# A planner for five engines: GpSimd waits for VectorE at the shared ports, a narrower last values product, and a new table of order

## The chip, the cores and the metric

The kernel runs on one core of a Trainium2 chip. A core has engines that each work through a queue of their own in order: PE (TensorE, matrix products), DVE (VectorE), ACT (ScalarE), POOL (GpSimd) and SP (SyncE, which issues the DMA transfers). They wait for each other by semaphores. The metric is the device time of one execution in microseconds, as the median of several runs.

## What is computed

Attention in which each row keeps only its 32 largest scores, and two dense blocks behind it. All is in 32-bit floating point.

```python
batch, n_heads, seq, head_dim = (2, 8, 576, 64)
scores = scale * np.matmul(q, k.transpose(0, 1, 3, 2))
kth = np.partition(scores, -top_k, axis=-1)[..., -top_k:-top_k + 1]      # top_k = 32
scores = np.where(scores >= kth, scores, -1000000000.0)
scores = scores - np.max(scores, axis=-1, keepdims=True)
attn = np.exp(scores)
attn = attn / (np.sum(attn, axis=-1, keepdims=True) + 1e-09)
x = np.matmul(attn, v)                      # laid out as 1152 tokens x 512
h = x @ w_in                                # 512 -> 2048
sp = np.where(h > 20.0, h, np.log1p(np.exp(np.minimum(h, 20.0))))
x = (h * np.tanh(sp)) @ w_out               # 2048 -> 512
h = x @ w2_in
return (h * (1.0 / (1.0 + np.exp(-h)))) @ w2_out
```

## The kernel before

The 1152 tokens are 9 tiles of 128 rows. For each tile the 8 heads are taken two at a time, so there are 36 attention steps of one tile and two heads; this text calls them **pairs** and numbers them from 1 in the order in which their reciprocals stand in DVE's queue. For a pair PE multiplies queries and keys, both split into a high and a low part (`scores`, L378, into `ps_att`); ACT or DVE copies the scores to `sc`; DVE finds the 32 largest of each row by four rounds of MAX8 (L394) and MATCH_REPLACE8 (L397) for each head. For the first six tiles ACT then computes the exponentials (L410) and DVE masks them and sums them up in one operation, the **mask** (L414, a SCALAR_TENSOR_TENSOR of 128x576 with a sum; two for a pair); for the last three tiles the mask is made ahead of the exponential instead, by ACT (L420) and a difference on POOL or DVE (L290, L292). The sum becomes `den`: a constant is added on ACT (L462) or POOL (L463), DVE takes the **reciprocal** (L466), ACT spreads it (L469). PE transposes the exponentials (`turn`, L439, nine 128x128 pieces), multiplies them by the values (`values`, L455 and L457), transposes the reciprocals (L471), and DVE multiplies both (L480), which gives the pair's x.

The two dense blocks take the tiles in the groups of `BLOCK1` and `BLOCK2`. Groups marked 'n' multiply in the native 32-bit form (an instruction gives two records in the trace), those marked 'r' split both sides into high and low parts and make three products (L630, L701, L808). Weights arrive as 64-bit floats and are turned into 32-bit ones once (`convert`: ACT at L505 and L517, POOL at L509 and L519). `split_unit` splits the activated values into two parts, the second a difference on POOL (L290) or DVE (L292).

Nothing of this is issued in the order in which the code is written. Every step is handed to `Plan.add` with its ways (an engine, a cost, a rank offset and a function), what it reads and writes, and the buffers that it uses. `Plan.emit` then runs a small clock for each engine and always emits the step that can start first, by rank among equals; this order is the order of the queues on the chip. The ranks come from tables: `TILES`, `DUE1` and `DUE2` give start times of tiles and groups, `FLEX`, `FLEX1`, `EARLY` and `OFF` offsets for kinds of steps and for the choice of the engine.

DVE and POOL share ports to the on-chip memory. The planner marks the operations that use them (`way[4]`: every POOL operation, and on DVE the two-elements-a-cycle copies, the differences and the masks) and does not let two of them overlap in its own clock (`port`). On the chip nothing keeps that order before the change: POOL starts as soon as its data are there.

## Time and profile before

| | |
|---|---|
| runs | 652.88, 656.01, 656.37 us; median 656.01 |
| profiled execution | span 654.1 us from the first to the last instruction; no other time of its own is given |
| PE busy | 606.1 us, 93% |
| DVE busy | 539.5 us, 82% |
| ACT busy | 476.3 us, 73% |
| POOL busy | 382.3 us, 58% |
| granted TensorE clock, mean | 0.987 |

The span lies inside the spread of the runs and 1.9 us below their median. A share of busy time is an average over the whole span; the kernel begins with attention alone and ends with matrix products alone, so the shares of its stretches differ.

### The profile page before, as it was taken

The page shows a single profiled execution, that of the slowest core. Times are in us where ns is not written, and L with a number is a line of the kernel's source. Part 1 is how long each engine was busy: PE and PEld are TensorE (multiplying, and loading weights), DVE is VectorE, ACT ScalarE, POOL GpSimd, SP SyncE. Part 2 cuts the span into 40 slices and gives each one's busy share as a digit, 9 for nine tenths or more (in the row PEclk, how much of TensorE's full clock was granted, in tenths as well). Part 3 has the DMA queues.
Part 4 walks back from the last instruction along what each step waited for, and adds up shares of the span by engine and source line. Part 5 has one row for each costly group of instructions (what it writes and reads, how often), then busy time and mean ns, then how long its engine had stood idle before and what let it go on. Part 6 is the DMA issues. An engine that isn't in the chain of part 4 may idle for free.

```text
span 654.1 us, 13089 instructions
## 1 busy us (share of the span) xinstructions
PE 606.1 (93%) x4536; PEld 537.0 (82%) x4536; DVE 539.5 (82%) x1106; ACT 476.3 (73%) x993; POOL 382.3 (58%) x334
## 2 busy tenths in 40 slices
PE   1298788999999999999999999999999999999997
PEld 1177667999999866668999878999988899999996
DVE  4999999997999999989999979979998234554550
ACT  6799999988699998988978666878777344332321
POOL 6898569761267888987549236556787233322221
PEclk9999967999999999999999999999999999999999
DMA  8987649898789868799999589875876998887752
GB/s 309 293 256 222 197 159 330 312 361 263 204 271 345 276 192 271 268 305 347 389 402 368 151 272 355 316 259 191 272 255 223 374 300 294 278 263 256 246 179 80
DMA packets 85650, 178.34 MB, mean 273 GB/s; under 512 B 8144, under 2 KB 29136, under 8 KB 85584
## 3 DMA queue, kind: packets, MB, share of 16 engines
q1 hardware_dynamic: 85584, 177.50, 80.4%
q8 instruction: 36, 0.59, 0.3%
q14 instruction: 30, 0.25, 0.1%
HBM read 138.94 MB, written 38.54 MB: 271 GB/s over the span
## 4 chain that ended last, share of the span: by engine, by line
PE 53%; DVE 16%; ACT 15%; DMA 7%; issue 4%; POOL 4%; SPq 1%; POOLq 0%; ACTq 0%
PE ps_h L630 20%; PE ps_y L701 12%; PE ps_y L808 11%; DVE m L394 6%; DVE rest L397 5%; ACT ws L505 4%; PE ps_att L378 3%; DMA wraw<-w1i 3%; PE ps_att L439 2%; PE ps_misc L455 2%; ACT wraw L517 2%; ACT pt L282 2%; ACT e L410 2%; DVE e L414 2%; POOL wraw L519 2%
## 5 line engine op out<-in xcount | busy, mean ns | idle before, releaser
L394 DVE MAX8 m<-rest 128x8 f32<-128x576 f32 x216 | 154.4, 745 | 0.1
L397 DVE MATCH_REPLACE8 rest<-m,rest 128x576 f32<-128x576 f32 x144 | 106.2, 741 | 0.0
L509 POOL TENSOR_TENSOR ws<-ws 128x512 int32<-128x512 int32 x64 | 86.7, 1359 | 28.9 <-ACT ws L505 27.2
L378 PE MATMUL ps_att<-kk,qs 128*128 128x288 f32 x320 | 72.8, 346 | 31.6 <-POOL kk L290 24.5
L282 ACT CAST ws<-wraw 128x512 fp32r<-128x512 f32 x93 | 57.4, 621 | 53.8 <-PE ps_h L630 25.3
L519 POOL TENSOR_TENSOR wraw<-wraw,ws 128x512 int32<-128x512 int32 x64 | 85.5, 1346 | 15.9 <-ACT wraw L517 11.0
L505 ACT ACTIVATE ws<-wide,zone 128x512 int32<-128x512 int16 x128 | 94.5, 779 | 0.0
L378 PEld LDWEIGHTS ps_att<-kk,qs 128*128 128x128 f32 x320 | 51.3, 205 | 43.2 <-POOL kk L290 26.0
L292 DVE TENSOR_TENSOR ws<-wraw,ws 128x512 fp32r<-128x512 f32 x65 | 58.9, 924 | 31.3 <-ACT ws L282 30.9
L630 PE MATMUL ps_h<-y,ws 128*128 128x256 f32 x576 | 75.3, 280 | 0.0
L630 PEld LDWEIGHTS ps_h<-y,ws 128*128 128x128 f32 x576 | 73.1, 188 | 2.7
L290 POOL TENSOR_TENSOR ws<-wraw,ws 128x512 fp32r<-128x512 f32 x44 | 57.6, 1318 | 27.3 <-ACT ws L282 14.8
L630 PE MATMUL ps_h<-xt,ws 128*128 128x256 f32 x576 | 72.8, 282 | 0.0
L701 PE MATMUL ps_y<-wide,ws 128*128 128x256 f32 x540 | 71.3, 283 | 0.0
L630 PEld LDWEIGHTS ps_h<-xt,ws 128*128 128x128 f32 x576 | 69.5, 188 | 1.5 <-issue 1.2
L290 POOL TENSOR_TENSOR wide<-th,wide 128x512 fp32r<-128x512 f32 x24 | 31.5, 1313 | 66.7 <-DVE wide L284 65.4
L701 PEld LDWEIGHTS ps_y<-wide,ws 128*128 128x128 f32 x540 | 66.5, 189 | 0.0
L808 PE MATMUL ps_y<-ws,wide 128*128 128x512 f32 x252 | 64.8, 396 | 0.0
L290 POOL TENSOR_TENSOR wide<-hs,wide 128x512 fp32r<-128x512 f32 x24 | 32.0, 1342 | 49.4 <-DVE wide L284 40.2
L439 PE MATMUL ps_att<-ident,e 128*128 128x128 f32 x324 | 52.6, 287 | 6.7 <-DVE e L414 3.9
L701 PE MATMUL ps_y<-hs,wraw 128*128 128x128 f32 x384 | 52.4, 286 | 2.2 <-ACT hs L670 2.2
L394 DVE MAX8 m<-sc 128x8 f32<-128x576 f32 x72 | 52.8, 747 | 1.3 <-ACT sc L282 0.7
(89 smaller groups left out, 1231.5 us busy)
## 6 DMA issues: line engine op xcount, KB each, us to landing
wraw<-w1i SPq DMA_DIRECT2D x64, 256.0 KB, 4.8
wraw<-w2i SPq DMA_DIRECT2D x64, 256.0 KB, 4.0
ws<-w1o_split SPq DMA_DIRECT2D x30, 512.0 KB, 5.1
ws<-w2o_split SPq DMA_DIRECT2D x28, 512.0 KB, 4.4
wraw<-w1o SPq DMA_DIRECT2D x48, 256.0 KB, 5.8
wide<-in_w1i_dram SPq DMA_DIRECT2D x16, 512.0 KB, 5.6
wide<-in_w1o_dram SPq DMA_DIRECT2D x16, 512.0 KB, 5.0
wide<-in_w2i_dram SPq DMA_DIRECT2D x16, 512.0 KB, 5.1
```

What stands on the lines that cost most here:

```text
L282: ways.append(("act", act_us(n, psum), act, lambda: nc.scalar.copy(get_out(), get_in())))
L290: ways.append(("pool", pool_us(n), pool, lambda: nc.gpsimd.tensor_tensor(out=get_out(), in0=get_a(), in1=get_b(), op=op)))
L378: nc.tensor.matmul(o, lhsT=l, rhs=r[:, f * SH:(f + 1) * SH], start=(i == 0), stop=(i == len(ops) - 1))
L394: add([("dve", 0.67, 0, lambda i=i, h=h, src=src: nc.vector.max(out=m8()[:, h, 8 * i:8 * i + 8], in_=src()[:, h]))], reads=srck, writes=[K ...
L397: add([("dve", 0.73, 0, lambda i=i, h=h, src=src: nc.vector.match_replace(out=rest()[:, h], in_to_replace=m8()[:, h, 8 * i:8 * i + 8], in_ ...
L439: nc.tensor.transpose(o[:, i, :], ef[:, (c + i) * P:(c + i + 1) * P], ident)
L505: add([("act", act_us(UNIT) + 0.14, 0, lambda i=i: nc.scalar.activation(pn()[:, i], top(), AF.Relu, scale=ONE16 - 2 * ONE16 * i, bias=zone))],
L509: ways = [("pool", pool_us(UNIT), 0, lambda: nc.gpsimd.tensor_tensor(out=se(), in0=pn()[:, 0], in1=pn()[:, 1], op=ALU.subtract))]
L519: add([("pool", pool_us(UNIT), 0, lambda: nc.gpsimd.tensor_tensor(out=w().bitcast(I32), in0=w().bitcast(I32), in1=se(), op=ALU.add))], rea ...
L630: nc.tensor.matmul(hp[:, c, :], lhsT=l, rhs=rr, start=(i == 0), stop=(i == len(ops) - 1))
L701: nc.tensor.matmul(yp[:, o, :], lhsT=l[:, d * P:(d + 1) * P], rhs=rr[:, c, :], start=(fc == 0 and k == 0 and o == 0), stop=last, skip_grou ...
L808: nc.tensor.matmul(op, lhsT=gg[:, c, i * P:(i + 1) * P], rhs=wt, start=(fc == 0 and k == 0), stop=(fc == NFC - 1 and k == len(ops) - 1))
```

## The change

Five things are edited. First, `Plan.emit` keeps the last port operation of DVE (`turn_of`), and when the next port operation that it emits is POOL's, that one gets a dependency on it (`order`, which adds a semaphore wait); in the planner's clock POOL may use the port 0.13 us after DVE's end. A DVE operation behind a POOL operation gets none. Second, the last chunk of the values product, which holds the tails of both heads, is two matmuls with 64 columns of weights, one for each head, instead of one with 128. Third, the split activations get three buffers of their own, `g`, instead of sharing `wide` with the arriving weights. Fourth, some costs and ranks in the planner change, and the scratch for DMA descriptors is set to 1024 bytes. Fifth, all numbers of the tables are new.

```diff
-TILES = [(19.37, 6.76), (46.36, 14.1), (106.73, 4.63), (204.37, 9.99), (225.06, 11.69), (258.55, 49.85), (345.98,
+TILES = [(-38.49, 10.5), (10.1, 9.21), (77.14, -12.91), (164.62, 9.79), (162.43, 9.24), (220.65, 45.49), (300.21,
...
-                 wraw=9, ws=8, hs=2, th=1, wide=3, y=2, o=2)
+    wraw=9, ws=8, hs=2, th=1, wide=3, g=3, y=2, o=2)
...
-        dma, hw, port = 0.0, 0.4, 0.0
+        dma, hw = 0.0, 0.4
+        port, turn_of = dict(dve=0.0, pool=0.0), None
...
-                    if way[4] and port > at:
-                        at, soon = port, soon and port <= free[e] + PORT
+                    if way[4] and port[e] > at:
+                        at, soon = port[e], soon and port[e] <= free[e] + PORT
...
-            fn()
+            done = fn()
             free[e] = end
-            if shared:
-                port = end
+            if shared and e == "dve":
+                port["pool"], turn_of = end + self.WAIT[e], done
+            elif shared:
+                port["dve"] = end
+                if turn_of is not None:
+                    self.order(done, turn_of)
+                    turn_of = None
...
+    def order(after, before):
+        tc.add_manual_dep(after.ins, before.ins.name, mybir.DependencyInfo(mybir.DependencyClass.Sync, mybir.DependencyReason.DATA),
+                          reason="port")
...
-                nc.tensor.matmul(av[:, r0:r1], lhsT=v[:, 2 * NM:].rearrange("p c e -> p (c e)"), rhs=pt()[:, NM, r0:r1],
-                                 start=False, stop=True, skip_group_check=True)
-        add([("pe", 1.35 * len(pp), 0, values)], reads=[K("pt", c) for c in range(0, NB, 3)] + [("v", b, p) for b, _, _ in pp],
+                for h in range(2):
+                    nc.tensor.matmul(av[h * D:h * D + D, r0:r1], lhsT=v[:, 2 * NM + h, :], rhs=pt()[:, NM, r0:r1],
+                                     start=False, stop=True, skip_group_check=True)
+        add([("pe", 1.25 if len(pp) == 1 else 1.32, 0, values)], reads=[K("pt", c) for c in range(0, NB, 3)] + [("v", b, p) for b, _, _ in pp],
...
-        add([("act", 0.11, 0, lambda: nc.scalar.add(den()[:, 0], den()[:, 0], tiny)),
+        add([("act", 0.2, 0, lambda: nc.scalar.add(den()[:, 0], den()[:, 0], tiny)),
...
-            rank=rank - 6, boost="wsplit")
+            rank=rank - (6 if g else 2), boost="wsplit")
...
-        hi = lambda: get(key, lambda: sbuf("wide", [P, 2 * UNIT + 2], F32R)[:, :2 * n].rearrange(
-            "p (t n) -> p t n", t=2))[:, 0]
+        hi = lambda: get(key, lambda: sbuf("g", [P, 2, UNIT], F32R)[:, :, :n])[:, 0]
...
-    nc = _bacc.Bacc("TRN2", target_bir_lowering=False, num_devices=1)
+    nc = _bacc.Bacc("TRN2", target_bir_lowering=False, num_devices=1, dynamic_dma_scratch_size=1024)
```

What the tables move is seen in the queues. Three places follow. Lines of the changed kernel are 12 to 14 higher: its L407, L410, L427, L480, L494 and L801 are L394, L397, L414, L466, L480 and L788 of before.

DVE's queue around pair 20, before: `m_2878` holds this pair's maxima, `m_3031` those of pair 21.

```order
L397 MATCH_REPLACE rest<-m_2878,rest 128x576
L394 MAX m_3031<-sc 128x8
L394 MAX m_2878<-rest 128x8
L394 MAX m_3031<-sc 128x8
L414 SCALAR_TENSOR_TENSOR e,den<-sc,m_2878,e 128x576
L788 SCALAR_TENSOR_TENSOR th<-th,ps_h 128x512
L397 MATCH_REPLACE rest<-m_3031,sc 128x576 x2
L394 MAX m_3031<-rest 128x8 x2
L397 MATCH_REPLACE rest<-m_3031,rest 128x576 x2
L414 SCALAR_TENSOR_TENSOR e,den<-sc,m_2878,e 128x576
L394 MAX m_3031<-rest 128x8
L466 RECIPROCAL den<-den 128x2
```

DVE's queue at the same place after the change: `m_2899` is pair 20, `m_3172` is pair 21.

```order
L407 MAX m_2899<-rest 128x8
L427 SCALAR_TENSOR_TENSOR e,den<-sc,m_2899,e 128x576 x2
L480 RECIPROCAL den<-den 128x2
L494 TENSOR_TENSOR x<-ps_misc,dt 128x128
L305 TENSOR_TENSOR xt<-x,xt 128x128
L297 COPY dt<-ps_att 128x128
L297 COPY sc<-ps_att 128x288 x2
L407 MAX m_3172<-sc 128x8
L494 TENSOR_TENSOR x<-ps_misc,dt 128x128
L410 MATCH_REPLACE rest<-m_3172,sc 128x576
L297 COPY sc<-ps_att 128x288
L407 MAX m_3172<-rest 128x8
```

Before, one mask of pair 20, then four replaces and two MAX of pair 21 with a product of th, then the other mask; now both masks stand together, and pair 21 begins behind them.

PE's queue at the very start, before (x24 are the scores of three pairs, eight each):

```order
L378 MATMUL ps_att<-kk,qs 128x288 x24
L439 MATMUL ps_att<-ident,e 128x128 x9
L471 MATMUL ps_att<-ident,x 128x128
L455 MATMUL ps_misc<-pt,v 64x128 x8
L457 MATMUL ps_misc<-pt,v 128x128
L722 MATMUL ps_h<-xt,wraw 128x128 x4
L378 MATMUL ps_att<-kk,qs 128x288 x4
```

The same after the change:

```order
L391 MATMUL ps_att<-kk,qs 128x288 x16
L452 MATMUL ps_att<-ident,e 128x128 x9
L485 MATMUL ps_att<-ident,x 128x128
L468 MATMUL ps_misc<-pt,v 64x128 x8
L471 MATMUL ps_misc<-pt,v 64x128 x2
L735 MATMUL ps_h<-xt,wraw 128x128 x4
L391 MATMUL ps_att<-kk,qs 128x288 x4
L735 MATMUL ps_h<-xt,wraw 128x128 x4
```

The scores of the third pair have moved behind the first pair's transposes, values and first weight product (L722, now L735).

POOL's queue near the start with its waits, before (the names in brackets are semaphores, one for each engine and DMA queue):

```order
L519 TENSOR_TENSOR wraw<-wraw,ws 128x512 [waits Pool_49] x2
L290 TENSOR_TENSOR kk<-kraw,kk 64x576 [waits DMAHW4_49,Activation_49,Pool_49]
L290 TENSOR_TENSOR kk<-kraw,kk 64x576 [waits Activation_49]
L290 TENSOR_TENSOR qs<-qraw,qs 128x256 [waits DVE_49,DMAHW5_49,PE_49,Pool_49]
L509 TENSOR_TENSOR ws<-ws 128x512 [waits Activation_49]
L290 TENSOR_TENSOR qs<-qraw,qs 128x256 [waits DMAHW6_49,PE_49,Activation_49]
L519 TENSOR_TENSOR wraw<-wraw,ws 128x512 [waits Pool_49]
```

The same place after the change:

```order
L523 TENSOR_TENSOR ws<-ws 128x512 [waits Activation_49]
L303 TENSOR_TENSOR kk<-kraw,kk 64x576 [waits DVE_49,DMAHW6_49,Activation_49,Pool_49]
L533 TENSOR_TENSOR wraw<-wraw,ws 128x512 [waits DVE_49,Pool_49]
L523 TENSOR_TENSOR ws<-ws 128x512 [waits Activation_49]
L303 TENSOR_TENSOR qs<-qraw,qs 128x256 [waits DMAHW5_49,Activation_49]
L533 TENSOR_TENSOR wraw<-wraw,ws 128x512 [waits Pool_49]
```

A difference of kk (DVE makes the one of the other head) and a weight sum, neither of which reads anything of DVE's, now also wait for DVE. In the whole queue 57 operations of POOL name DVE in their waits, before 51; 21 dens are added on POOL where it was 12, and 13 differences of split activations where it was 48; 22 differences of e where it was 18, and 52 of ws where it was 44.

## Rows read from the trace of the kernel before

**Rows 1.** The page's head: span, and busy time of PE with its load path and others.
```profile
span 654.1 us, 13089 instructions
PE 606.1 (93%) x4536; PEld 537.0 (82%) x4536; DVE 539.5 (82%) x1106; ACT 476.3 (73%) x993; POOL 382.3 (58%) x334
```
**Rows 2.** Stretches: from:to, length, busy of each engine (count), granted clock, DMA share, GB/s.
```profile
0.00:120.00 120.00, 81.24 (x534) 68.75 (x535) 109.32 (x234) 108.09 (x226) 92.89 (x83) 0.93 0.78 253
120.00:240.00 120.00, 118.94 (x995) 109.15 (x994) 116.06 (x257) 108.04 (x226) 72.29 (x72) 1.00 0.83 280
240.00:280.00 40.00, 37.57 (x226) 25.23 (x226) 36.56 (x77) 37.05 (x78) 35.63 (x29) 1.00 0.82 268
280.00:520.00 240.00, 237.99 (x1869) 212.41 (x1869) 217.43 (x456) 179.39 (x400) 145.71 (x126) 1.00 0.86 298
520.00:600.00 80.00, 80.00 (x622) 77.30 (x621) 37.71 (x56) 29.20 (x44) 24.66 (x19) 1.00 0.83 277
```
**Rows 3.** The chain that ended last, four of its pieces: start, us, what.
```profile
129.78 2.68 PE ps_h L630 x24
...
299.02 1.72 PE ps_y L808 x4
...
515.25 18.37 PE ps_h L630 x156
...
639.16 11.17 PE ps_y L808 x48
```
**Rows 4.** Timeline of PE, one pair's values: start, us, operation, count.
```profile
199.00 1.09 PE L455 MATMUL ps_misc<-pt,v 128*64 128x128 f32 x16
200.02 0.49 PE L457 MATMUL ps_misc<-pt,v 128*128 128x128 f32 x2
200.35 1.06 PE L701 MATMUL ps_y<-hs,wraw 128*128 128x128 f32 x8
```
**Rows 5.** Timeline of DVE: the reciprocals of pairs 11 and 36.
```profile
149.00 0.15 DVE L466 RECIPROCAL den<-den 128x2 f32<-128x2 f32 x1
...
507.11 0.17 DVE L466 RECIPROCAL den<-den 128x2 f32<-128x2 f32 x1 [1.33 <-POOL den L463]
```
**Rows 6.** Timeline of DVE between the two masks of pair 20.
```profile
260.96 1.46 DVE L414 SCALAR_TENSOR_TENSOR e<-sc,m,e 128x576 f32<-128x576 f32 x1 [0.82 <-ACT e L410]
...
264.41 1.41 DVE L394 MAX8 m<-rest 128x8 f32<-128x576 f32 x2
265.74 0.07 DVE L397 MATCH_VALUE_LOAD rest<-m,rest 128x8 f32 x1
...
267.18 0.94 DVE L414 SCALAR_TENSOR_TENSOR e<-sc,m,e 128x576 f32<-128x576 f32 x1
...
268.73 0.14 DVE L466 RECIPROCAL den<-den 128x2 f32<-128x2 f32 x1
```
**Rows 7.** Waits of DVE from 280 to 520: us in total, times, longest.
```profile
DVE sc L284 <- PE ps_att L378: 5.3, 4, 2.0
...
DVE x L480 <- PE ps_misc L457: 3.0, 4, 1.1
...
DVE den L466 <- POOL den L463: 1.7, 2, 1.3
```
**Rows 8.** Masks and POOL's sums: ns min/median/max by line, and the masks' group with mean.
```profile
L414 DVE SCALAR_TENSOR_TENSOR e<-sc,m,e x48: 795/814/1955, 22.0 to 384.7; 128x576 f32<-128x576 f32 x48
...
L414 DVE SCALAR_TENSOR_TENSOR e<-sc,m,e 128x576 f32<-128x576 f32 x48 | 48.1, 1028 | 0.8 <-ACT e L410 0.8
...
L509 POOL TENSOR_TENSOR ws<-ws x64: 1267/1281/1795, 11.0 to 291.7; 128x512 int32<-128x512 int32 x64
```
**Rows 9.** Timeline of PE: the third pair's scores at the start.
```profile
31.86 2.73 PE L378 MATMUL ps_att<-kk,qs 128*128 128x288 f32 x8 [8.83 <-POOL kk L290]
```
**Rows 10.** Waits: POOL's dens in the whole span, PE for weights from 120 to 480.
```profile
POOL den L463 <- DVE e L414: 18.0, 6, 6.9
...
PE ps_y L808 <- POOL wraw L519: 0.5, 1, 0.5
```

More of the change, by code (lines that the diff above doesn't have):

```diff
@@ L30 @@
 BLOCK2 = [([0, 1], 'n'), ([2], 'n'), ([3, 4], 'r'), ([5, 6], 'r'), ([7, 8], 'r')]
[L32 to L35 removed]
+TILES = [(-38.49, 10.5), (10.1, 9.21), (77.14, -12.91), (164.62, 9.79), (162.43, 9.24), (220.65, 45.49), (300.21,
+    17.89), (724.13, -16.34), (656.61, -8.72)]
@@ L37 @@
+DUE1 = [(54.47, 54.88), (68.81, 49.55), (170.23, 47.88), (254.51, 23.7), (324.83, 185.25), (1002.33, 11.91)]
+DUE2 = [(192.96, 67.23), (242.59, 124.44), (449.05, 137.95), (1029.53, 152.0), (1089.45, 830.82)]
 SBUF_BUFS = dict(kraw=1, kk=5, v=5, qraw=2, qs=2, sc=4, rest=1, e=1, pt=2, m8=10, bias=10, den=8, x=3, dt=2, xt=1,
-                 wraw=9, ws=8, hs=2, th=1, wide=3, y=2, o=2)
+    wraw=9, ws=8, hs=2, th=1, wide=3, g=3, y=2, o=2)
 PSUM_BUFS = dict(att=2, misc=1, h=3, y=2)
-FLEX = dict(khi=-199.43, klo=-179.86, qhi=-300.0, qlo=65.82, whi=259.95, wlo=-153.31, ghi=-62.92, glo=163.54,
-            hs=286.73, mk=-58.0, se=-300.0, den=105.07, y=271.68, sc=-47.47, pt=57.06, dt=-238.16, xlo=98.83)
@@ L43 @@
-FLEX1 = dict(khi=245.84, klo=30.36, qhi=-26.57, qlo=179.72, whi=-172.94, wlo=-208.13, ghi=-191.1, glo=300.0, hs=19.48,
-             mk=8.23, se=None, den=-282.09, y=None, sc=252.9, pt=None, dt=239.76, xlo=-232.84)
-EARLY = 553.02
-OFF = dict(kload=578.07, qload=135.46, k=16.71, q=-13.88, sp=314.62, sc=197.87, bias=39.06, e=246.77, tp=342.92,
-           pt=330.03, av=-14.23, x=487.41, den=300.22, dw=35.2, dp=222.21, xt=191.17, m=-75.12, cload=96.71,
-           cpn=-97.42, cse=5.37, cw=-99.8, cmid=-37.21, wload=572.6, wsplit=-171.63, wstore=206.7, g=-82.77, hs=-40.2,
-           y=-31.25, th=709.1)
+FLEX = dict(khi=-2304.26, klo=-1729.17, qhi=4585.01, qlo=-1836.37, whi=-557.43, wlo=4059.12, ghi=208.36,
+    glo=348.77, hs=-2437.93, mk=1501.27, se=1901.19, den=557.47, y=545.22, sc=-90.82, pt=288.52, dt=-4945.63,
+    xlo=4398.82)
@@ new lines @@
+FLEX1 = dict(khi=2169.2, klo=301.89, qhi=1509.44, qlo=1221.56, whi=1936.6, wlo=-179.34, ghi=-6043.64,
+    glo=-1109.55, hs=1112.11, mk=4042.01, se=None, den=96.95, y=None, sc=2045.53, pt=None, dt=3320.09,
+    xlo=-380.99)
+EARLY = 2775.67
+OFF = dict(kload=2225.49, qload=4412.15, k=-120.17, q=-150.24, sp=388.0, sc=612.22, bias=22.71, e=452.34,
+    tp=1842.03, pt=3573.68, av=-3190.48, x=628.58, den=5197.79, dw=375.46, dp=1276.78, xt=1759.28, m=-794.24,
+    cload=1514.82, cpn=-148.0, cse=-1893.7, cw=-193.27, cmid=293.34, wload=-280.81, wsplit=-1020.77,
+    wstore=-630.61, g=-522.71, hs=-590.32, y=2878.12, th=827.44)
@@ L78, with __init__ @@
     TABLE = 1.3
-    def __init__(self, bufs):
+    def __init__(self, bufs, order=None):
         self.columns = {}
+        self.order = order
         self.bufs, self.steps = bufs, []
@@ L267, in psum @@
         return ps.tile(shape, F32, tag="ps_" + tag, name="ps_" + tag, bufs=PSUM_BUFS[tag])
-    plan = Plan({**SBUF_BUFS, "keep": KEEP, **{"ps_" + t: n for t, n in PSUM_BUFS.items()}})
+    def order(after, before):
+        tc.add_manual_dep(after.ins, before.ins.name, mybir.DependencyInfo(mybir.DependencyClass.Sync, mybir.DependencyReason.DATA),
+                          reason="port")
+    plan = Plan({**SBUF_BUFS, "keep": KEEP, **{"ps_" + t: n for t, n in PSUM_BUFS.items()}}, order)
     add = plan.add
@@ L359, in attention @@
             if len(pp) > 1:
-                add([("pool", 0.6, 0, lambda mk=mk: nc.gpsimd.memset(mk().bitcast(F32), 0.0))], writes=[q], uses=[(q, "qs")],
+                add([("pool", 0.5, 0, lambda mk=mk: nc.gpsimd.memset(mk().bitcast(F32), 0.0))], writes=[q], uses=[(q, "qs")],
                     rank=rank - 6)
@@ L405, in attention @@
                 continue
-            add([("act", 0.1, 0, lambda i=i, col=col, by=by: nc.scalar.mul(bias()[:, i], m8()[:, :, col:col + 1], by))],
+            add([("act", 0.12, 0, lambda i=i, col=col, by=by: nc.scalar.mul(bias()[:, i], m8()[:, :, col:col + 1], by))],
                 reads=[K("m8", h, col // 8) for h in range(2)], writes=[K("bias", i)],
@@ L634, in split_unit @@
     def split_unit(key, n, U, src, skeys, suses, r):
-        hi = lambda: get(key, lambda: sbuf("wide", [P, 2 * UNIT + 2], F32R)[:, :2 * n].rearrange(
-            "p (t n) -> p t n", t=2))[:, 0]
-        add(copy_ways(n, hi, src, dve="ghi", twice=True), reads=skeys, writes=[key + (0,)], uses=suses + [(key, "wide")],
+        hi = lambda: get(key, lambda: sbuf("g", [P, 2, UNIT], F32R)[:, :, :n])[:, 0]
+        add(copy_ways(n, hi, src, dve="ghi", twice=True), reads=skeys, writes=[key + (0,)], uses=suses + [(key, "g")],
             rank=r, boost="g")
         add(tt_ways(n, lambda: T[key][:, 1], src, hi, ALU.subtract, dve="glo"), reads=skeys + [key + (0,)],
-            writes=[key + (1,)], uses=suses + [(key, "wide")], rank=r, boost="g")
-        return ([key + (0,), key + (1,)], [(key, "wide")],
+            writes=[key + (1,)], uses=suses + [(key, "g")], rank=r, boost="g")
+        return ([key + (0,), key + (1,)], [(key, "g")],
                 lambda: tuple(T[key][:, i].rearrange("p (u n) -> p u n", u=U) for i in range(2)))
```

5 lines of the change are left out of this document (1 added, 4 removed).

## The prediction

> **What bounds the kernel now.** I read the page's busy times first [rows 1]: PE is busy 606.1 of 654.1 us, DVE 539.5, ACT 476.3, POOL 382.3. The stretches [rows 2] then say that the 48 us without a matmul are not spread out. PE stands 38.8 us of the first 120; from 120 to 520 us it stands only 5.5 in all (1.1, 2.4 and 2.0), and from 520 to 600 not at all. DVE is the other full engine: busy 109.3 us of the first 120 and 116.1 of the next. So two queues run side by side: DVE finds the 32 largest scores of one pair after another (a row tile and two heads; 36 pairs, numbered by their reciprocals in DVE's queue), and PE, in a fixed order, has matrix products to do until the next pair's masked exponentials are ready.
>
> For such a couple one number per pair is useful: **the path through pair k**, which is the time at which DVE has finished the pair's masks plus all the PE work that stands in PE's order from that pair's transposes on. No schedule ends its matmuls before the longest path. I take the moment from the reciprocal that follows the masks on DVE, and the PE work from counts of matmuls at the spacing they have when nothing is waited for. The chain of work shows it [rows 3]: 0.118 us for a split product of 256 columns (156 in 18.37), 0.233 for one of 512 (48 in 11.17), 0.112 for a native record of 128 columns (24 in 2.68), 0.43 for one of 512 (4 in 1.72); a native instruction is two records. Put between them, a native instruction of 256 columns is 0.43, a scores matmul (288 columns, one record) 0.133, a transpose (128) 0.11. The values products of one pair take 1.35, from 199.00 to 200.35 [rows 4].
>
> At pair 20 there remain 1728 split products of 256 columns (203.9), 288 of 512 (67.1), 32 native instructions of 512 (27.5), 20 of 256 (8.6), 64 of 128 (14.2), 120 scores (16), 170 transposes (18.7) and 16 whole and two part pairs of values (25): 381 us. With the reciprocal at 268.73 [rows 6] the path is 649.9. Counted in the same way the path through pair 11 is 149.00 plus 488.8, 637.8, and through pair 36, the last, 507.11 plus 143.1, 650.2 [rows 5]. The last matmul ends at 650.33 (639.16 and 11.17 [rows 3]). So the count closes within half a microsecond, and it shows where 12 us entered: **between pair 11 and pair 20**. There DVE took 119.7 us for operations that add up to 110.8 at their undisturbed spacing (0.667 us a MAX8, two from 264.41 to 265.74; 0.72 a replace with its load, two from there to 267.18 [rows 6]).
>
> **The new order.** At pair 11 DVE has 1.1 us more ahead of it than before (one MAX8 and a kk difference more, a cast fewer), and 489.1 us of PE work remain: 150.1 plus 489.1 is 639.2, 1.4 later. At pair 20 the order changes what counts. Before, the second mask of pair 20 stands behind four replaces and two MAX8 of pair 21; in the trace it starts at 267.18, 6.2 us after the first at 260.96 [rows 6]. Now both masks stand side by side ahead of pair 21. In the whole queue up to there, nine top-k operations fewer stand ahead (6.2 us), with a few small ones 6.5 in all: 234.8 for 241.3. From pair 11 that is 103.2 us of work in place of 110.8; with the same 8.9 us of lag (119.7 less 110.8), pair 20 is done at 262.2. The PE work left is 376.5 (four native 256-column instructions fewer, 8 scores more, the values further on and cheaper, below). Path: 638.7, against 649.9. At pair 36 the DVE work from pair 20 on is 210.6 for 209.9, and before it took 238.4 us, a lag of 28.5. If all that lag stays, pair 36 is done at 501.3, with 145.7 us of PE work behind it: 647.0. But 8.3 of the 28.5 us are DVE waiting for PE (scores 5.3, values 3.0 [rows 7]), and that shrinks when PE is less far behind.
>
> So the last matmul falls between 639.2 (pair 11 decides, all of those 8.3 us vanish) and 647.0 (pair 36 decides, none). I take the middle, 643.1, since only some of these waits are of PE's making alone.
>
> **The wait at the port.** Before, a mask on DVE takes 814 ns in the median, 1028 in the mean and 1955 at most, and a POOL operation of 128x512 takes 1281 [rows 8]: 48 masks lose 10.3 us, 0.21 each. Now a POOL operation that the planner puts behind such a DVE operation waits for its end; a DVE operation that it puts behind a POOL operation gets no wait and can still be held. Bounds: nothing gained (all the losses are of the second kind), or all of what lies ahead of pair 11, 22 masks, 4.7, and of pair 20, 40 masks, 8.6. I take 2 us off the path, nearer to nothing, because few POOL operations are concerned: the new queue names DVE in 57 of some 310 operations, 17 of them dens and 4 differences of g, which wait for data, so that some 36 are left for the port. The Trainium skill says more (SBUF — State Buffer, section SBUF: two separate sides): the shared pair of ports is an exclusive lock, whoever starts first has it for the whole instruction and the other is blocked. By it a mask that meets a fresh POOL operation takes 0.81 plus 1.28, 2.09 us, and the trace's longest, 1.955, agrees; it speaks against the change, for a lock serves both in turn and the wait only moves from DVE to POOL, so that by the rule the 2 us go, and the sum is 649.
>
> **Edits of little or no cost.** The tail of the values product becomes two matmuls of 64 columns of weights in place of one of 128. A pair's 16 narrow records take 1.02 us and the two wide ones 0.33 [rows 4]; four narrow ones at 0.064 are 0.26, and between 0 and 0.1 us a pair is gained, at most 4 us in 40 tails; 2.6 is already in the counts. At the start 16 instead of 24 scores matmuls stand ahead of the first transposes; the last eight of those waited 8.83 us for POOL's kk and started at 31.86 [rows 9]. The first x comes some 9 us earlier, and I count that as nothing: DVE is the queue of that stretch, and pair 11 stays where it is; if DVE had no such work to go on with, it would be worth those 9. The separate g buffers, the smaller DMA scratch and the costs in the tables issue nothing. 35 differences of g go from POOL to DVE, at most 28 us at a mask's 0.81; 12 of them lie ahead of pair 36 and are in its sum, the other 23 fall where DVE is busy 37.7 us of 80 [rows 2], and without that cover they would add up to 19.
>
> **The sum.** 643.1 less 2.0 for the port is 641.1 for the last matmul; the profile ends 3.8 us behind it: 644.9, against its own span of 654.1. The median of the runs is 1.9 us above that span, so 646.8: I say **647**.
>
> **Rivals.**
> *More than that.* The port losses vanish whole and the later lag shrinks: pair 11 decides at 639.2 less 4.7, and with 3.8 and 1.9 that is 640. For it speaks that DVE is busy nearly without a break; against it, that waits on one side only are added.
> *The den step eats it.* POOL adds the constant to 21 denominators instead of 12, and the reciprocal on DVE waits for each. Before, two of twelve made DVE stand, 1.7 us in all, 1.3 the longest [rows 7]. If half of 21 do, at 0.85, it is 9 us: 656, no change. It decides as soon as POOL comes more than one MAX8 (0.667) late to a den.
> *POOL late with weights: slower.* POOL's queue stands whole behind each wait, the operations on weights, kk and qs with it. Before, its 12 dens waited 18.0 us for DVE's masks [rows 10], 1.5 each; 9 more make 13.5 us, and 15 port waits up to the last conversions, at a mask's 0.81, make 12. POOL is idle 79 us of the first 280, but only 4.4 from 240 to 280 [rows 2], where it converts the last weights. If all 25 us pile up there, 21 come too much, matmuls on raw weights wait for them, and it is 668. It decides when the waits of that stretch exceed those 4.4 us. Against it: from 120 to 480 us PE stood for a converted weight only 0.5 us [rows 10], and most new waits lie where POOL has time.
> *The edit does nothing at the port.* Then the order alone gives 649.
>
> **Chances.** The forecast with its neighbour, order alone, 641 to 652.7: 0.55. More: 0.17. Den or other new waits, no change: 0.16. Slower by the weights: 0.12. Half a per cent, 3.3 us, is about what a measurement of this kernel can tell from no change; so faster 0.72, same 0.16, slower 0.12. The range reaches from 638 (the first rival) to 658, and leaves out the last rival and the outer part of the first, under 2 in 10. The likeliest case's own range is 641 to 652.
>
> **What would show it.** In the profile after: the two masks of pair 20 side by side, its reciprocal at 258 to 263 us; pair 11's reciprocal at 146 to 151; PE's idle time from 120 to 520 below 5.5 us; the mean of the masks between 0.85 and 1.0 us. Wrong would make me: DVE standing at reciprocals for POOL over 5 us in all, PE waiting for wraw, or pair 11 later than 152.

## The result and the profile after

The changed kernel takes **647.46 us** in the median of 4 runs (642.01 to 650.23); before, in the same session, 655.84 (652.88 to 656.37). The ratio is 0.9874, with a 95% interval from 0.9838 to 0.991: faster, by 8 us, and the forecast of 647 stands within half a microsecond. Its two parts do not: the new order, with the narrow tail in its counts, was to bring 7 us and the port waits 2. The experiments show nearly the reverse.

The page of the profile after, its span and busy times, answers to [rows 1]; this execution took 642.01 us, 1.8 more than its span:

```profile
span 640.2 us, 13237 instructions
PE 592.8 (93%) x4616; PEld 527.9 (82%) x4616; DVE 528.0 (82%) x1121; ACT 476.9 (74%) x991; POOL 338.0 (53%) x319
```

PE has nearly the same products to do (80 records more, all of the narrow tail) and is busy 13.3 us less: they follow each other more closely, so that its busy time is no measure of its work. DVE is busy 11.5 us less, POOL 44. The stretches, which answer to [rows 2] (busy time and operations of each engine, then the granted TensorE clock, the DMA share and GB/s):

```profile
0.00:120.00 120.00, 79.74 (x592) 68.94 (x593) 109.50 (x242) 109.18 (x222) 92.28 (x92) 0.94 0.83 265
120.00:240.00 120.00, 117.58 (x992) 106.87 (x992) 113.89 (x254) 107.14 (x226) 73.41 (x77) 1.00 0.86 286
240.00:280.00 40.00, 39.05 (x280) 27.80 (x279) 33.92 (x76) 38.22 (x77) 30.93 (x29) 1.00 0.89 295
280.00:520.00 240.00, 239.95 (x1947) 216.97 (x1946) 210.48 (x450) 186.59 (x413) 138.75 (x122) 1.00 0.85 300
520.00:600.00 80.00, 80.00 (x605) 75.85 (x604) 44.46 (x77) 26.00 (x41) 2.58 (x2) 1.00 0.83 281
```

From 120 to 520 us PE stands 2.42, 0.95 and 0.05 us, together 3.4 where it was 5.5. Of the first 120 us busy time says little: PE is busy 79.74 us there for 81.24, but starts 592 records for 534. How far a kernel has come is better seen by its pairs, in the second table below. The DVE groups of masks, of differences of weights (`ws`, the low part of a split weight) and of reciprocals (busy us, mean ns; idle time ahead of them and what ended it) answer to [rows 7, 8]:

```profile
L427 DVE SCALAR_TENSOR_TENSOR e<-sc,m,e 128x576 f32<-128x576 f32 x48 | 41.6, 884 | 1.2 <-ACT e L423 0.9
L305 DVE TENSOR_TENSOR ws<-wraw,ws 128x512 fp32r<-128x512 f32 x57 | 41.5, 734 | 30.2 <-ACT ws L295 29.8
L480 DVE RECIPROCAL den<-den 128x2 f32<-128x2 f32 x36 | 5.5, 152 | 0.9 <-ACT den L476 0.5 <-POOL den L477 0.3
```

A mask takes 884 ns in the mean for 1028, and a difference of weights 734; before it was 924, in a row of the same view:

```profile
L292 DVE TENSOR_TENSOR ws<-wraw,ws 128x512 fp32r<-128x512 f32 x65 | 58.9, 924 | 31.3 <-ACT ws L282 30.9
```

At reciprocals DVE waited 0.3 us for POOL. What PE waited for from 12 to 140 us (in total, times, longest):

```profile
PE ps_att L391 <- POOL kk L303: 11.3, 1, 11.3
PE ps_y L714 <- ACT bias L419: 7.6, 1, 7.6
PE ps_y L735 <- POOL wraw L533: 4.0, 3, 3.2
```

The second row names a tiny ACT operation that DVE's maxima release; PE's weight loads (PEld) of the same line waited 7.7 us for POOL's `wraw`, so both stand for the same wait for a converted weight.

DVE around pair 20, in order of time (start, duration), answers to [rows 6]:

```profile
255.61 0.87 DVE L427 SCALAR_TENSOR_TENSOR e<-sc,m,e 128x576 f32<-128x576 f32 x1
256.41 0.81 DVE L427 SCALAR_TENSOR_TENSOR e<-sc,m,e 128x576 f32<-128x576 f32 x1
...
257.56 0.17 DVE L480 RECIPROCAL den<-den 128x2 f32<-128x2 f32 x1 [0.34 <-POOL den L477]
257.64 0.27 DVE L494 TENSOR_TENSOR x<-ps_misc,dt 128x128 f32<-128x128 f32 x1
260.44 0.29 DVE L305 TENSOR_TENSOR xt<-x,xt 128x128 fp32r<-128x128 f32 x1 [2.52 <-ACT xt L295]
261.40 0.29 DVE L297 COPY dt<-ps_att 128x128 f32<-128x128 f32 x1 [0.67 <-PE ps_att L485]
262.70 0.82 DVE L297 COPY sc<-ps_att 128x288 f32<-128x288 f32 x2 [1.01 <-PE ps_att L391]
```

Pair 20 is done at 257.56 instead of 268.73, as the order promised. But the reader should look at what follows: DVE has nothing of pair 21 to go on with. It stands 2.52, 0.67 and 1.01 us, the last of them for pair 21's scores, and begins that pair only at 262.70. Before, pair 21 was half searched when pair 20 was done. The chain's last piece of PE ends at 636.5 (625.32 and 11.20), 3.7 us ahead of the end of the span.

### The profile page after: what moved, and what is told of

It is laid out like the page before. It is cut to its first block, busy times and chain, and to the rows that moved or that the text cites. A ratio compares the mean times of both kernels' runs of the same rounds, so it can differ in the third digit from the quotient of the medians.

```text
span 640.2 us, 13237 instructions
## 1 busy us (share of the span) xinstructions
PE 592.8 (93%) x4616; PEld 527.9 (82%) x4616; DVE 528.0 (82%) x1121; ACT 476.9 (74%) x991; POOL 338.0 (53%) x319
## 4 chain that ended last, share of the span: by engine, by line
PE 73%; ACT 13%; DMA 7%; DVE 4%; POOL 1%; issue 1%; SPq 0%; POOLq 0%; ACTq 0%; DVEq 0%
PE ps_h L644 26%; PE ps_y L714 16%; PE ps_y L821 15%; PE ps_att L391 5%; PE ps_misc L468 5%; ACT ws L519 4%; PE ps_att L452 4%; DMA w2i<-wraw 2%; ACT wraw L531 2%; DVE m L407 2%; DMA wide<-in_w1o_dram 2%; DVE rest L410 2%; DMA qraw<-in_qh_dram 1%; ACT sc L295 1%; ACT pt L295 1%
## 5 line engine op out<-in xcount | busy, mean ns | idle before, releaser
L407 DVE MAX8 m<-rest 128x8 f32<-128x576 f32 x216 | 154.2, 745 | 0.1
L410 DVE MATCH_REPLACE8 rest<-m,rest 128x576 f32<-128x576 f32 x144 | 106.1, 741 | 0.0
L533 POOL TENSOR_TENSOR wraw<-wraw,ws 128x512 int32<-128x512 int32 x64 | 81.6, 1283 | 15.0 <-ACT wraw L531 3.1
L391 PE MATMUL ps_att<-kk,qs 128*128 128x288 f32 x320 | 67.7, 334 | 22.9 <-POOL kk L303 18.5
L523 POOL TENSOR_TENSOR ws<-ws 128x512 int32<-128x512 int32 x64 | 81.8, 1289 | 9.5 <-ACT ws L519 6.3
L303 POOL TENSOR_TENSOR ws<-wraw,ws 128x512 fp32r<-128x512 f32 x52 | 66.6, 1296 | 26.2 <-DVE ws L297 7.4
L714 PE MATMUL ps_y<-g,ws 128*128 128x256 f32 x540 | 70.1, 280 | 0.0
L305 DVE TENSOR_TENSOR ws<-wraw,ws 128x512 fp32r<-128x512 f32 x57 | 41.5, 734 | 30.2 <-ACT ws L295 29.8
L714 PEld LDWEIGHTS ps_y<-g,ws 128*128 128x128 f32 x540 | 65.3, 188 | 0.7 <-issue 0.7
L821 PE MATMUL ps_y<-ws,g 128*128 128x512 f32 x252 | 65.4, 398 | 0.0
L407 DVE MAX8 m<-sc 128x8 f32<-128x576 f32 x72 | 53.0, 746 | 4.2 <-ACT sc L295 4.1
L714 PEld LDWEIGHTS ps_y<-hs,wraw 128*128 128x128 f32 x384 | 48.2, 198 | 8.3 <-POOL wraw L533 7.7
L410 DVE MATCH_REPLACE8 rest<-m,sc 128x576 f32<-128x576 f32 x72 | 53.1, 740 | 0.0
```

The source lines that it names most:

```text
L303: ways.append(("pool", pool_us(n), pool, lambda: nc.gpsimd.tensor_tensor(out=get_out(), in0=get_a(), in1=get_b(), op=op)))
L391: nc.tensor.matmul(o, lhsT=l, rhs=r[:, f * SH:(f + 1) * SH], start=(i == 0), stop=(i == len(ops) - 1))
L407: add([("dve", 0.67, 0, lambda i=i, h=h, src=src: nc.vector.max(out=m8()[:, h, 8 * i:8 * i + 8], in_=src()[:, h]))], reads=srck, writes=[K ...
L410: add([("dve", 0.73, 0, lambda i=i, h=h, src=src: nc.vector.match_replace(out=rest()[:, h], in_to_replace=m8()[:, h, 8 * i:8 * i + 8], in_ ...
L523: ways = [("pool", pool_us(UNIT), 0, lambda: nc.gpsimd.tensor_tensor(out=se(), in0=pn()[:, 0], in1=pn()[:, 1], op=ALU.subtract))]
L533: add([("pool", pool_us(UNIT), 0, lambda: nc.gpsimd.tensor_tensor(out=w().bitcast(I32), in0=w().bitcast(I32), in1=se(), op=ALU.add))], rea ...
```

## The experiments

All times are medians, in us. The kernel before ran beside each group: 653.99 beside the first four rows, 654.18 beside "waits from 19 to 25 only" and the last three rows, 653.77 beside the other four. The ratios are not those of the medians, so that a difference between two kernels comes out a little otherwise by them.

| kernel | time | ratio to before, 95% |
|---|---|---|
| changed kernel, again | 646.98 | 0.9856 to 0.9913 |
| its queues, no port waits | 651.81 | 0.9922 to 0.9981 |
| queues of before, with waits | 649.52 | 0.9907 to 0.995 |
| changed, old wide tail | 648.17 | 0.9876 to 0.9927 |
| changed, waits up to pair 19 only | 652.27 | 0.9944 to 0.9994 |
| changed, waits from pair 19 on | 647.78 | 0.9874 to 0.9923 |
| changed, waits from 19 to 25 only | 647.52 | 0.9875 to 0.9918 |
| changed, DVE waits for POOL too | 647.5 | 0.9881 to 0.994 |
| before, mask of pair 20 moved | 654.46 | 0.9986 to 1.0017 |
| new order alone (no waits, wide tail) | 655.1 | 0.9999 to 1.0032 |
| before, waits from pair 19 on | 652.72 | 0.9969 to 1.0 |
| new code, old tables | 664.22 | 1.0125 to 1.0169 |

The times at which DVE took some pairs' reciprocals, read from the timeline of each profile:

| kernel | pair 8 | 20 | 22 | 25 | 36 |
|---|---|---|---|---|---|
| before | 111.8 | 268.7 | 296.0 | 355.7 | 507.1 |
| before, with waits | 108.3 | 264.1 | 290.7 | 349.1 | 500.7 |
| new order alone | 110.1 | 259.9 | 301.0 | 353.0 | 499.6 |
| no port waits | 112.0 | 261.8 | 303.0 | 354.5 | 500.7 |
| waits to 19 | 108.7 | 259.5 | 300.9 | 352.3 | 498.5 |
| waits from 19 | 113.8 | 264.1 | 303.8 | 352.6 | 499.1 |
| waits 19 to 25 | 111.0 | 261.2 | 300.4 | 348.8 | 495.1 |
| changed | 107.0 | 257.6 | 296.5 | 344.7 | 491.1 |

**The parts of the change.** The changed kernel was run again, to set its parts against:

> The changed kernel once more, as the measure for the three that run beside it. Expected 0.987 of the kernel before, within 0.984 to 0.991. A repeat that lands above 0.993 would say that the first comparison was lucky.

It gave 646.98. Then its queues with the call that adds the dependency left out:

```diff
                 port["dve"] = end
                 if turn_of is not None:
-                    self.order(done, turn_of)
                     turn_of = None
```

> The changed kernel with the same queues, but without the waits of GpSimd for VectorE. If the order is the cause (my theory), the time rises by 2 us at most, to about 0.990 of the kernel before; the masks' mean rises from 884 ns towards 1030 and the reciprocal of pair 20 comes 1 to 4 us later than 257.6. If the waits are the cause (first rival), nearly all is lost: 0.996 to 1.00. If the lock only moves the wait from one engine to the other (second rival), the time stays within 1 us of the changed kernel although the masks slow down.

651.81: the waits are worth 4.8 us by the medians and 4.3 by the ratios (0.9951 and 0.9885), about twice the forecast's 2; the two intervals leave some 2 to 7. The ratio lies just below the range that the expectation gave to the waits as the cause. The mirror image gives the queues of before the same waits, in before's own planner:

```diff
             if shared:
                 port = end
+                if e == "dve":
+                    turn_of = done
+                elif turn_of is not None:
+                    self.order(done, turn_of)
+                    turn_of = None
```

> The kernel before with the same queues, and the waits of GpSimd for VectorE added. Order theory: 0.995 to 1.00, the masks' mean falls from 1028 ns to below 900, and pair 20 still ends late, at 264 us or more. Wait theory: 0.990 or less. A third outcome, slower than before (above 1.003), would say that this order, made without the wait in the planner's clock, loses more by GpSimd standing than DVE gains.

649.52: 4.5 us, without any new order. The ratio, 0.9928, lies between the two outcomes that the expectation named, and the masks fell to 949 ns and not below 900. Third, the changed kernel with the old tail of the values product:

```diff
-                for h in range(2):
-                    nc.tensor.matmul(av[h * D:h * D + D, r0:r1], lhsT=v[:, 2 * NM + h, :], rhs=pt()[:, NM, r0:r1],
+                nc.tensor.matmul(av[:, r0:r1], lhsT=v[:, 2 * NM:].rearrange("p c e -> p (c e)"), rhs=pt()[:, NM, r0:r1],
...
```

> The changed kernel with the old tail of the values product: one matmul of 128 columns of weights in place of two of 64, the rest of the queues the same. By the spacing of the rows before, 0.07 us more a tail, 40 tails: 2.6 us of PE work, all of it ahead of the end, so 2 to 3 us slower than the changed kernel. If the narrow ones cost what the wide one did, no difference.

648.17: the narrow tail is worth 1.2 us, less than the 2 to 3 expected, with intervals that overlap. Against the queues of before with waits, 649.52, this kernel shows what the rest of the change, the order above all, brings where the waits are there: 1.4 us, which these intervals can't tell from nothing either.

**Was pair 20 the place?** In the queues of before, only the second mask of pair 20 is moved, right behind the first (`emit` collects its steps in a list and runs them at its end):

```diff
+        emitted.insert(to, emitted.pop(b))      # b: the second mask; to: behind the first
+        for _, _, fn in emitted:
+            fn()
```

> The kernel before with one VectorE operation moved: the second mask of pair 20 stands right behind the first, ahead of one operation of the hidden layer, four replaces and two MAX8, and nothing else changes. The prediction's path through pair 20 (649.9 us, of which 12 were said to enter between pair 11 and pair 20) should then shorten by what the mask comes earlier, less where the next pairs decide: transposes of pair 20 at 263 to 264 in place of 268.3, and 3 to 5 us faster, 649 to 651 in place of 654. Rival: TensorE was not waiting for that mask, as it ran values products up to 268.27 us and stood only 1.1 us from 240 to 280; then nothing, 653 to 655.

654.46, no change (0.9986 to 1.0017). In its trace the masks start 1.8 us apart, and DVE is done with them at 263.7 instead of 268.1:

```profile
260.05 1.84 DVE L429 SCALAR_TENSOR_TENSOR e<-sc,m,e 128x576 f32<-128x576 f32 x1
...
261.82 1.92 DVE L429 SCALAR_TENSOR_TENSOR e<-sc,m,e 128x576 f32<-128x576 f32 x1
```

But PE, in the same trace, comes to the transposes that need the second mask when it has gone through what stands ahead of them in its queue:

```profile
264.49 1.95 PE L823 MATMUL ps_y<-wraw,th 128*128 128x512 f32 x4 [0.26 <-DVE th L803]
266.38 0.69 PE L470 MATMUL ps_misc<-pt,v 128*64 128x64 f32 x16
...
268.24 0.82 PE L454 MATMUL ps_att<-ident,e 128*128 128x128 f32 x6
```

and before the change it came there at the same time, 0.03 us later:

```profile
268.27 0.82 PE L439 MATMUL ps_att<-ident,e 128*128 128x128 f32 x6
```

So nobody was waiting for that mask. (PE's idle time of 1.1 us, which the expectation puts between 240 and 280, is that from 120 to 240; from 240 to 280 it is 2.4 [rows 2].) The forecast took a late mask for a late engine.

**Where the waits pay.** The same queues and waits, but given only up to, or only from, the moment at which the planner has emitted 19 reciprocals:

```diff
     def order(after, before):
+        if len(pairs) >= 19:      # the other kernel: < 19
+            return
```

> The changed kernel with its queues as they are, but GpSimd waits at the shared ports only up to the reciprocal of pair 19; from there on no such wait. Without any wait the same queues gave 651.8 us, with all of them 647.0. If the waits pay where masks meet the last weight sums and differences behind pair 20 (87.1 us from reciprocal 20 to 25 with waits, 92.7 without), this one loses nearly all of that: 651 to 652, reciprocals 20 to 25 again some 92 us apart. If they pay in the first 120 us, where VectorE is the queue, it keeps all: 647, masks behind pair 20 longer without a price. Half and half: 649.5.

> The changed kernel with its queues as they are, but GpSimd waits at the shared ports only from the reciprocal of pair 19 on. If the waits pay behind pair 20: 647 to 648, reciprocal 8 at 112 us and 20 at 262 as without waits, but 20 to 25 only 87 us apart. If they pay in the first 120 us: 651 to 652. Half and half: 649.5; the two halves should then add up to the 4.8 us of the whole.

652.27 and 647.78: the early waits bring nothing, the late ones all of it, to within the 2 us or so that the intervals leave. Of the 24 early waits 14 stand at dens, which wait for their masks in any case. A third kernel has only the waits that are given between pairs 19 and 25, 15 of the 55 (the expectation says 16):

```diff
+        if not 19 <= len(pairs) < 25:
+            return
```

> The changed kernel with its queues as they are, and of the 55 waits at the shared ports only the 16 that are given out between the reciprocals of pair 19 and pair 25; nearly all of them stand behind differences of weights, g and xt on VectorE, not behind masks. If the 9 differences of weights from 260 to 360 us (1462 ns each without waits, 806 with) are the whole gain, this gives all of it: 647 to 648, pair 25 some 87 us behind pair 20. If the waits behind pair 25 carry half of it: 649.5. If it was the run of the first 120 us after all: 651 to 652.

647.52: **15 waits give the whole gain**, as far as the intervals tell (0.9875 to 0.9918, with all waits 0.9856 to 0.9913). Four stand behind differences of weights, four behind operations on `g`, four behind differences of `xt`, and three behind masks, two of these at dens again. Which of the 15 carry it was not tried. What they keep apart is seen best in one place. Without waits, DVE and POOL in one timeline:

```profile
304.30 1.30 POOL L532 TENSOR_TENSOR wraw<-wraw,ws 128x512 int32<-128x512 int32 x1
304.67 3.17 DVE L304 TENSOR_TENSOR ws<-wraw,ws 128x512 fp32r<-128x512 f32 x2 [0.27 <-ACT ws L294]
305.55 1.74 POOL L522 TENSOR_TENSOR ws<-ws 128x512 int32<-128x512 int32 x1
...
307.38 1.60 POOL L532 TENSOR_TENSOR wraw<-wraw,ws 128x512 int32<-128x512 int32 x1
```

and the same operations with the 15 waits:

```profile
302.81 1.61 DVE L309 TENSOR_TENSOR ws<-wraw,ws 128x512 fp32r<-128x512 f32 x2
...
304.84 1.29 POOL L537 TENSOR_TENSOR wraw<-wraw,ws 128x512 int32<-128x512 int32 x1 [1.57 <-issue]
306.09 1.28 POOL L527 TENSOR_TENSOR ws<-ws 128x512 int32<-128x512 int32 x1
307.45 1.29 POOL L537 TENSOR_TENSOR wraw<-wraw,ws 128x512 int32<-128x512 int32 x1
```

Two differences on DVE take 1.61 us where they took 3.17, while POOL stands 1.57 us and gets half of that back, since its own operations fall from 1.74 and 1.60 to 1.28 and 1.29. The differences of weights from 260 to 360 us, without waits, with the late ones, and with the 15:

```profile
L304 DVE TENSOR_TENSOR ws<-wraw,ws 128x512 fp32r<-128x512 f32 x9 | 13.0, 1462 | 0.4 <-ACT ws L294 0.3
```

```profile
L309 DVE TENSOR_TENSOR ws<-wraw,ws 128x512 fp32r<-128x512 f32 x9 | 6.9, 780 | 0.3 <-ACT ws L299 0.2
```

```profile
L309 DVE TENSOR_TENSOR ws<-wraw,ws 128x512 fp32r<-128x512 f32 x9 | 7.0, 802 | 0.0
```

Nine operations give 6.0 us back. Without waits they take, from the shortest over the median to the longest (in ns):

```profile
L304 DVE TENSOR_TENSOR ws<-wraw,ws x9: 681/1565/1933, 281.6 to 346.2; 128x512 fp32r<-128x512 f32 x9
```

From pair 20 to pair 25 it is 92.7 us without waits, 92.8 with the early ones, 88.5 with the late ones, 87.6 with the 15.

In the old order the place is another one. There DVE's differences of weights meet POOL less in that stretch, as the row of before from 260 to 360 us says:

```profile
L292 DVE TENSOR_TENSOR ws<-wraw,ws 128x512 fp32r<-128x512 f32 x18 | 14.1, 809 | 0.5 <-ACT ws L282 0.4
```

But its masks of the first 150 us take 1093 ns, and of the 25 waits up to pair 19 only 3 stand at dens. The late waits alone, with before's queues (the edit is the one above, `< 19`):

> The queues of the kernel before, with the waits at the ports only from the reciprocal of pair 19 on (all of them gave 649.5 us for 654). If the place is the same as in the new order, where VectorE does differences of weights behind pair 20, it keeps the gain: 649 to 650. If here the masks of the first 120 us carry it (16 masks at 1136 ns in the mean before, 17 at 1020 with all waits, pair 11 at 145.8 for 149.0), it keeps a third or less: 652 to 654.

652.72, against 649.52 with all waits: two thirds of that gain are early here, by subtraction, as the early waits alone were not run in this order. The masks up to 150 us before the change, then with all waits, then with the late ones:

```profile
L414 DVE SCALAR_TENSOR_TENSOR e<-sc,m,e 128x576 f32<-128x576 f32 x22 | 23.4, 1093 | 0.0
```

```profile
L424 DVE SCALAR_TENSOR_TENSOR e<-sc,m,e 128x576 f32<-128x576 f32 x22 | 20.7, 972 | 0.0
```

```profile
L428 DVE SCALAR_TENSOR_TENSOR e<-sc,m,e 128x576 f32<-128x576 f32 x22 | 23.5, 1096 | 0.0
```

**Does DVE gain by waiting as well?** The other half of the lock, added to the changed kernel:

```diff
             if shared and e == "dve":
+                if pool_of is not None:
+                    self.order(done, pool_of)
+                    pool_of = None
                 port["pool"], turn_of = end + self.WAIT[e], done
             elif shared:
-                port["dve"] = end
+                port["dve"], pool_of = end, done
```

> The changed kernel with its queues as they are, and the other half of the waits added: a VectorE operation also waits for the GpSimd operation that the planner puts ahead of it at the shared ports. If the port is a lock that serves both in turn, this wait only replaces one that is there: 647, masks at a mean near 0.85 us, and VectorE's idle time grows by what its operations shorten. If what counts is that overlapping operations lengthen one another, the masks and differences get shorter by 0.05 to 0.1 us in the mean and it is 645 to 647. If VectorE now stands for whole GpSimd operations (1.28 us) where it would have lost less by overlapping, or for ones that come late, it is slower: 650 to 655.

647.5, nothing more. Its groups on DVE show why:

```profile
L308 DVE TENSOR_TENSOR ws<-wraw,ws 128x512 fp32r<-128x512 f32 x57 | 39.0, 690 | 33.6 <-ACT ws L298 28.6 <-POOL ws L306 1.9 <-POOL ws L526 1.2
L430 DVE SCALAR_TENSOR_TENSOR e<-sc,m,e 128x576 f32<-128x576 f32 x48 | 38.2, 814 | 8.0 <-POOL ws L526 2.5 <-POOL kk L306 1.9 <-POOL wraw L536 1.3
```

Now no mask and no difference is lengthened at all (814 and 690 ns), 3.4 and 2.5 us less busy than in the changed kernel. But DVE stands 6.8 us more ahead of the masks and 3.4 more ahead of the differences: on this side the wait only takes the place of the longer operation.

**The order alone, and the tables.** No waits and the wide tail:

> The changed kernel with no wait at the ports and with the old wide tail of the values products: the new order by itself, with nothing else of the change. The prediction gave the order alone 649, 7 us faster than the 656 before. The other reading: VectorE has nothing left of pair 21 when pair 20 is done early, stands for scores, and pair 22 is done as late as before, so that the order by itself brings nothing: 652 to 655.

655.1, against 654.18 before: the order alone brings nothing (0.9999 to 1.0032). (It is not quite alone: the `g` buffers, the costs and the DMA scratch are those of the change.) The forecast's 649 has the tail's 2.6 in it, so that its value for this kernel is 651.6. DVE's differences of weights from 260 to 360 us and PE's waits up to 140 us in its trace:

```profile
L304 DVE TENSOR_TENSOR ws<-wraw,ws 128x512 fp32r<-128x512 f32 x9 | 13.0, 1461 | 0.2
```

```profile
PE ps_y L712 <- ACT bias L418: 6.9, 1, 6.9
...
PE ps_y L733 <- POOL wraw L531: 3.1, 2, 2.6
```

The stretch from 280 to 360 us, here and then with the changed kernel's narrow tail and the 15 waits, shows what the order costs without them:

```profile
280.00:360.00 80.00, 76.33 (x603) 68.82 (x602) 78.15 (x150) 66.74 (x140) 59.57 (x48) 1.00 0.92 335
280.00:360.00 80.00, 79.84 (x652) 73.45 (x651) 75.29 (x160) 70.67 (x151) 62.21 (x54) 1.00 0.95 352
```

Before the change PE is busy 78.85 of these 80 us and 37.57 of the 40 ahead of them; with the order alone it is 76.33 and 39.54. So in these profiles PE stands 2 us less ahead of 280 us and 2.5 us more behind it, where DVE's differences meet POOL.

Last, the code of the change with the tables of before (the code as changed, `TILES` to `OFF` as they were):

> The code of the changed kernel (waits, narrow tail, two port times in the planner, separate g buffers) with the tables of numbers of the kernel before, so that the planner makes a third order. If the gain is in the waits and the tail, and the order is worth nothing by itself: 647 to 650. If the tables had to be found again for the new rules (some ranks and costs stand against others): 655 or more.

664.22, slower than both. Pair 36 is done at 518.2 us there, 11 later than before. Which of the planner's new costs and rules does it was not taken apart; the run shows only that the code needs tables found for it.

## Why the forecast held, and where its steps failed

**The new order: 7 us forecast with the tail, 2.2 measured with it (651.81) and nothing without; with the waits, 1.4 without the tail.** The step that failed is "it shows where 12 us entered: between pair 11 and pair 20". The sum adds the PE work from a pair's transposes on, 381 us for pair 20, to the pair's reciprocal, at 268.73. But before the change PE began these transposes six microseconds earlier, those of the first head while the second mask was still to come:

```profile
262.48 0.55 PE L439 MATMUL ps_att<-ident,e 128*128 128x128 f32 x3
```

So 6.2 of the 12 us are work that the path counts as still ahead when PE had already done it: the 381 us from 262.48 on end at 643.5. Taken from the first transposes in the same way, pair 11 (148.27) gives 637.1 and pair 36 (506.93) 650.0, so that about as much enters behind pair 20 as ahead of it. For the same reason such a path is no bound that every schedule must keep. Nor does it say that PE waited for pair 20: PE's own idle time was there to be read, 1.1 us from 120 to 240 and 2.4 from 240 to 280 [rows 2], and the moved mask settles it: no change.

The next step failed too: "if all that lag stays, pair 36 is done at 501.3". The number came out (499.6 with the order alone), but it hides what lies between. From pair 20 to 22 the new order takes 41.1 us where before it took 27.3, since pair 21 begins from nothing, and pair 22 is 5 us later than before. "I take the middle, 643.1" was the wrong end: 499.6 and the 145.7 us behind it are 645.3, with 3.8 a span of 649.1, and the profile of the order alone has 650.7. So pair 36 decides. Between that span and before's 654.1 there still are 3.4 us, of which the medians show nothing: before's profile stood 1.9 above the later medians of the same kernel, since 654.1 and 1.8 are 655.9, and this one 2.5 below its own. PE's wait for converted weights near 90 us, 7 us in one piece and 3 in smaller ones, is new and comes with the order, as it is there without waits; whether it eats what the earlier x brings was not tried.

**The wait at the port: 2 us forecast, 4.8 measured (4.3 by the ratios)**, inside its bounds of 0 to 8.6. The masks did get shorter, from 1028 to 884 ns; but in the new order that is not where the time came from. The prediction priced the masks alone, because they were the rows that it looked at. The differences of weights use the same port, were lengthened as much (924 ns in the mean before, 681 at the shortest without waits), and nine of them stand between pairs 20 and 25 in the new order, where DVE is the queue. Its "nearer to nothing, because few POOL operations are concerned" was wrong as a way of counting: 15 of 55 suffice.

The Trainium skill (SBUF — State Buffer, section SBUF: two separate sides) says that whoever starts first holds the shared ports for the whole instruction. For DVE's longest operations the traces agree: a difference takes at most 1.933 us without waits, and 0.68 plus a POOL operation's 1.28 is 1.96. The prediction drew from it that a wait on POOL's side "only moves", and its rival "the edit does nothing at the port" rested on that. What fell is this conclusion, not the rule: the wait does move, from DVE, which PE waits for, to POOL, which has time to spare. Where it moves within DVE, in the kernel with both waits, it is worth nothing.

**The narrow tail: 2.6 us in the counts, at most 4.** It measured 1.2 with the waits, and 3.3 without them (651.81 and 655.1, of two sessions; 4.3 by the ratios): the size is right to within what these runs tell. In the traces a pair's values take 1.24 us where they took 1.27 to 1.35. But something else goes with it. The products of split values with 256 columns, some 1700 in every kernel, are counted at 0.118 us throughout; in the changed kernel two of their three groups start 114 ns apart in the median, in all 3 us less than before. With the order alone it is 118 again, but so it is with the narrow tail in the old tables. Why they close up stays open, and the 3 us are in no term of the forecast.

**The end and the sum.** The span ends 3.7 us behind the last matmul (3.8 forecast). Adding up what was measured, from 654.2: 0.9 for the order, 3.3 off for the tail and 4.8 off for the waits give 647.0; these are steps from one kernel to the other, so they must come out. Taken the other way, by 653.99, 649.52, 648.17 and 646.98, they are 4.5 for the waits, 1.4 for the order and 1.2 for the tail: the order may be worth something only where the waits are there (the intervals don't settle it), and in both ways the waits are the largest part. The forecast came to the same number from 656 with 7 and 2. Its order was 5 us too good, its waits 3 too small, and its starting point 2 too high; a right sum is no proof of its terms.

**The rivals.** *More* (640) is not reached; the fastest run is 642.01. *The den step* is refuted by 0.3 us of waiting. *POOL late with weights* is there in the wrong place: PE does stand for `wraw`, near 90 us, but with or without waits, and from 240 to 280 us POOL is busy 30.93 of 40 us, less than before. *Nothing at the port* is refuted in both orders.

**What was to show it.** Pair 20's reciprocal at 257.56 lies 0.4 ahead of the forecast's 258 to 263, pair 11's at 145.5 lies 0.5 ahead of 146 to 151 (in the second profile of the same kernel, 259.0 and 147.8); PE's idle time and the masks' mean are inside. Of the signs of being wrong one showed: PE waiting for `wraw`, 4.0 us near 90 us and, in the row that names ACT's `bias`, 7.6. The signs of being right as good as came true, and the cause behind the first was still wrong: they tested that the order had changed, not that somebody had been waiting.

## What to carry to other kernels

Before a late operation gets a price, look at the engine that reads it: if that engine works up to the moment when the operation is done, moving it earlier is worth nothing, and one kernel with that one operation moved shows it. Two engines that share a port are worth keeping apart by a wait on the engine that has time to spare, at the places where the other one is behind; here 15 such waits did it, and a wait on both sides gave nothing more. A new order can bring such meetings where the old one had few: look at the port again behind each reordering. Price every kind of operation that uses the port, by its mean against its shortest, stretch by stretch.

## What was not expected of the hardware

Meeting at the port lengthens the operations of both engines in turn: of POOL's sums of 128x512 above, the one that began 0.37 us ahead of DVE's differences kept its 1.30 us, the two that began beside them took 1.74 and 1.60. A short operation loses the most for its length: a difference of 128x128 took 0.29 us in the changed kernel, and at the same place, with the order alone, 1.40:

```profile
262.40 1.40 DVE L304 TENSOR_TENSOR xt<-x,xt 128x128 fp32r<-128x128 f32 x1 [2.19 <-ACT xt L294]
```

The first 120 us differ from execution to execution by more than most edits are worth. Pair 8 is done at 107.0 us in the first profile of the changed kernel and at 110.1 in the second; the granted clock of that stretch is 0.94 in the one and 0.90 in the other. The latest is the kernel with the late waits, at 113.8, with 0.87:

```profile
0.00:120.00 120.00, 78.64 (x531) 66.61 (x532) 104.36 (x229) 104.75 (x214) 88.60 (x86) 0.87 0.78 249
```

In the other kernels with the new queues the order is much the same (0.94 with 107.2 and 108.7, 0.91 with 110.1 and 111.0, 0.90 with 112.0, 0.89 with 112.0). Those without early waits lie at 110.1 to 113.8, those with them at 107.0 to 112.0, so that a part of this may be the waits'; at the end of the kernel nothing of it is seen (652.27 with the early waits alone). The granted clock here is a mean over its two levels, 1.2 and 2.4 GHz, as a share of the upper one. From 40 to 100 us PE is busy only 10 to 16 us of each 20 there, and that is where the clock falls most, in single slices to 0.72; from 120 us on it is 0.98 to 1.00 in every stretch read. Which of the two comes first, a late pair or a low clock, these runs don't tell. Parts of 2 us were therefore compared by medians and not by two profiles.
